# One pool of eight single PSUM banks in place of 3 + 4 + 1, with finer waits of the output projection

## The chip, the cores and the metric

The kernel runs on one core of a Trainium2 chip. The metric is the device time of one execution in microseconds (us). The core has a matrix engine (PE), a vector engine (DVE), a scalar engine (ACT), a further vector engine (POOL) and a queue for transfers (SP); they run side by side and wait for each other through semaphores. Matrix results land in PSUM, which this kernel uses as eight banks of 128 partitions x 512 float32; only after DVE or ACT has copied a bank out (evacuated it) can PE write it again.

## The reference, cut to what matters

Four layers on one sequence of 2048 rows of 576 columns: A, B, A, B, each added to its input after a normalization.

```python
def _A_ref(x, wqkv, wo):            # 32 heads of 18, window of 8 keys at distance 2
    ...
    logits = jnp.where(mask, jnp.einsum('bhsd,bhswd->bhsw', q, kg) * scale, -1e9)
    attn = _softmax(logits, axis=-1)
    o = jnp.einsum('bhsw,bhswd->bhsd', attn, vg)
    return o.transpose(0, 2, 1, 3).reshape(B, S, D) @ wo

def _B_ref(x, mem0, Wq, Wk, Wv, Wo, seg_len):   # 32 heads of 128, memory of 8 rows, segments of 32
    mem = mem0
    for s in range(n_seg):
        h = jnp.concatenate([mem, xs], axis=1)
        q, k, v = ...                            # three projections of h
        p = _softmax(jnp.where(mask, scores, -1e9), axis=-1)
        o = jnp.einsum('bhqk,bhke->bhqe', p, v)
        o = jnp.einsum('bhte,hed->btd', o, Wo)
        mem = o[:, :M, :].copy()                 # the next segment's memory
        outs.append(o[:, M:, :])

x = x + _A_ref(_layernorm(x), A_wqkv, A_wo)
x = x + _B_ref(_layernorm(x), B_mem0, B_Wq, B_Wk, B_Wv, B_Wo, B_seg_len)
x = x + _A_ref(_layernorm(x), A_wqkv, A_wo)
x = x + _B_ref(_layernorm(x), B_mem0, B_Wq, B_Wk, B_Wv, B_Wo, B_seg_len)
```

Layer B is a recurrence: the memory that a segment of 32 rows leaves is read by the next segment.

## The kernel before

All four layers run interleaved. Both B layers go on together as two "lanes": step t works on segment t of the first B layer and on segment t-6 of the second, so there are 64 + 6 = 70 steps (and one last projection). The A layers supply B with tiles of 64 rows, 32 tiles for each of two layers, 64 in all, so that two steps go by for two A tiles (one of each layer).

Every piece of work is recorded as an operation with an engine (or a choice of two: `AD_` is ACT or DVE), a cost, a priority and the buffers that it takes and frees. A planner (`_Plan.run`) then plays these through time with its own costs and writes the instructions out in the order that it finds; the numbers in `PR` are priorities. Each engine works through its written order strictly one instruction after the other.

A step of B (`b_step`) consists of:

- `qk`: eleven groups of up to three heads; a group fills one bank with queries and keys, and a copy by ACT or DVE takes it to SBUF (L731 and L733 on PE);
- `vpass`: values, two banks for each of three blocks (L776);
- `scores`: four of them (memory rows "m" and segment rows "x", each in two halves r = 0, 1), a softmax behind each (L809, L821; then L667 to L686 on DVE, ACT and POOL);
- `pv_m`, twice (r = 0, 1), and `pv_x`, once: probabilities times values (L845, L883). PE works in four groups of 32 rows of its array, and each group writes a bank of its own, so that four banks are taken at a time. The evacuations put the result into the SBUF tile `OT`, which has four parts c = 0 to 3 of eight heads each. `pv_x` of step t is used by the projection of step t+1;
- `oproj`: the output projection into one bank `psY`, as eight operations k = 0 to 7 of four heads each (L917); heads of operation k lie in part c = k mod 4, half r = k div 4, of `OT`;
- `mem_out`: three small copies on DVE from that bank into `hT`, the next step's input (L937 to L939). The first `qk` group of the next step waits for them. `x_out` adds the other rows to the residual (L959).

A tile of A (`a_tile`) has a normalization (L407), projections to q, k, v (L476), products on POOL, logits (L525), a softmax, and then `spread` (L550): 20 matmuls in four row groups copy the probabilities of 32 heads to the 18 rows of each head, into the tile `big`, which is then multiplied by v and summed on DVE and POOL, and projected (L582).

PSUM before is cut into three pools: `r` has three single banks, for everything but what follows; `o4` is one tile of four banks, for `pv_m`, `pv_x` and `spread`; `y` is one bank for `oproj`:

```python
self.pl.pool("r", [pp.tile([P, 512], F32, name=f"r{i}") for i in range(3)])
self.pl.pool("o4", [pp.tile([P, 4, 512], F32, name="o4")])
self.pl.pool("y", [pp.tile([P, 5, W80], F32, name="psY")])
```

So `pv_m`, `pv_x` and `spread` follow each other through one buffer: the next of them starts when all evacuations of the one before are done. `spread` takes it twice for a tile, with 16 and with 4 matmuls. Its evacuations copy one of five column blocks each, and read all four banks for it; those of `pv_x` copy one bank each; that of `pv_m` copies 64 columns of all four banks in one instruction.

The writing layer adds semaphore waits wherever two instructions of different engines touch the same tile; for a tile in PSUM it does so also where both only read it.

Of the kernel before, what the change touches and what calls it, by code (L numbers as in the profile page):

```python
# [16 lines left out]
P = 128  # L17
# [38 lines left out]
class _Plan:  # L56
# [36 lines left out]
    def run(self, log=None):  # L93
# [21 lines left out]
        while left:  # L115
            moved = True
            while moved:
                moved = False
                for e, heap in ready.items():
# [3 lines left out]
                    pick = None  # L123
                    while heap:
# [13 lines left out]
                        if all(len(self.pools[p]) >= k for p, k in need.items()):  # L138
                            pick = o
                            break  # L140
                        skipped.append(it)
# [63 lines left out]
class _K:  # L205
# [37 lines left out]
    def setup(self):  # L243
# [187 lines left out]
    def a_tile(self, layer, j, dep, due, span):  # L431
# [4 lines left out]
        def pr(f):  # L436
            return due - span * (1.0 - f)
# [108 lines left out]
        def spread(ps, c0, nb):  # L546
            for c in range(nb):
                for g in range(NQ):
                    q4 = slice(g * AH, (g + 1) * AH)
                    nc.tensor.matmul(ps.t[:, g, c * P:(c + 1) * P], lhsT=self.epadT[q4, c0 + c, :],  # L550
                                     rhs=e_.t[q4].rearrange("p w t -> p (w t)"), start=True, stop=True, skip_group_check=True)
        ps = pl.buf("o4")
        b = pl.op("PE", 0.35, lambda e, ps=ps: spread(ps, 0, 4), pr(Q[4]), [o], acq=[ps], uses=[e_], mode="R")
        evs = []
        for c in range(5):
            if c == 4:
                ps = pl.buf("o4")
                b = pl.op("PE", 0.1, lambda e, ps=ps: spread(ps, 4, 1), pr(Q[4] + 0.02), [b], acq=[ps], uses=[e_], mode="R")
            evs.append(pl.op(AD_, _evac(512),
                             lambda e, c=c, ps=ps: self.copy(e, big.t[:, c].rearrange("p w (g t) -> p g w t", g=NQ),  # L560
                                                             ps.t[:, :, c % 4 * P:(c % 4 + 1) * P].rearrange("p g (w t) -> p g w t", w=AW)),
                             pr(Q[4] + 0.01 * c), [b], uses=[ps, big]))
        mus = []
        for c0, nb in ((0, 2), (2, 2), (4, 1)):
            mus.append(pl.op("DVE", 0.15 + 0.3 * nb,
                             lambda e, c0=c0, nb=nb: self.tt(e, big.t[:, c0:c0 + nb], big.t[:, c0:c0 + nb], win(vT.t, c0, nb), ALU.mult),
                             pr(Q[5]), evs[c0:c0 + nb] + [got[2], got[2, "h"]], uses=[big, vT], lk=True))
# [268 lines left out]
    def pv_m(self, t, r, prio):  # L836
        nc, pl = self.nc, self.pl
        ps, (pt, dep), V = pl.buf("o4"), self.PT["m", r], self.vs(t)
# [253 lines left out]
```

## Time and profile before

| | |
|---|---|
| median of three runs | 2525.39 us (2518.47 to 2528.63) |
| profiled execution | 2515.65 us, its span 2513.9 us |
| granted clock of PE | 0.989 |
| busy: PE, DVE, ACT, POOL | 2178.0, 1449.9, 1173.8, 845.5 us |
| matmuls | 70664 |

The page shows for each engine its busy time; the time between is idle, and a further view gives, for each engine and line, what ended the idle time ("waited for"), with the total, the number of waits and the longest. "issue" there means that the engine waited for nothing that the profile shows. In the view of instructions in order of time, a row has its start and length in us, engine, line, operation, `written<-read` tiles, shape, a count, and in brackets the idle time before it with its releaser. The tile `o4` has the name `o` there, since numbers at the end of a name are left out; `r` stands for any of the three banks.

### The profile page before, as it was taken

The numbers are of one execution on the slowest core, as the hardware profiler recorded it, in microseconds if no ns is written. First come the engines' busy times: TensorE is split into PE (matmuls) and PEld (weight loads), VectorE is DVE, ScalarE is ACT, GpSimd is POOL, SyncE is SP. The second block draws the span as 40 slices with busy tenths as digits, with TensorE's granted clock in tenths as the row PEclk, the third lists the DMA queues.
The fourth block names the chain that finished last, engine by engine and source line by source line (L and its number), as shares of the span: only waits on it lengthen the run. The fifth ranks groups of instructions, "written<-read, shape, count | busy, mean of one in ns | idle before, by whom it ended". The sixth has DMA issues, their size and how long they took to land.

```text
span 2513.9 us, 153081 instructions
## 1 busy us (share of the span) xinstructions
PE 2178.0 (87%) x70664; PEld 1864.2 (74%) x70664; DVE 1449.9 (58%) x3510; ACT 1173.8 (47%) x2633; POOL 845.5 (34%) x1205
## 2 busy tenths in 40 slices
PE   0178889999999999999988999999999999999988
PEld 0167777778878777787877877788777887777776
DVE  1046656666566666666566666566566666665554
ACT  0034444455545554545544554445545455444443
POOL 4232442333333333233333333323333333332320
PEclk9999989999999999999999999999999999999999
DMA  7732333334344333333333433433343433322210
GB/s 249 206 118 85 114 99 99 98 106 121 110 117 117 108 103 114 103 109 103 113 114 113 121 103 96 116 100 106 105 119 108 122 112 107 99 81 64 64 50 10
DMA packets 231399, 270.11 MB, mean 107 GB/s; under 512 B 42340, under 2 KB 227236, under 8 KB 229220
## 3 DMA queue, kind: packets, MB, share of 16 engines
q1 hardware_dynamic: 227508, 241.44, 33.1%
q0 software_dynamic: 3248, 18.88, 2.2%
q8 instruction: 552, 9.04, 1.5%
q14 instruction: 91, 0.75, 0.1%
HBM read 244.10 MB, written 16.12 MB: 104 GB/s over the span
## 4 chain that ended last, share of the span: by engine, by line
PE 69%; DVE 12%; ACT 7%; issue 6%; SPq 3%; POOL 2%; DMA 1%; ACTq 0%; DVEq 0%; POOLq 0%
PE r L731 23%; PE psY L917 15%; PE r L776 8%; PE r L733 6%; PE r L476 6%; DVE big L235 3%; ACT big L233 3%; SPq L308 3%; PE o L883 3%; DVE r L668 2%; DVE nmx L667 2%; PE o L845 2%; PE r L582 2%; ACT OT L233 2%; ACT em L670 2%
## 5 line engine op out<-in xcount | busy, mean ns | idle before, releaser
L731 PE MATMUL r<-hT,wk 128*128 128x80 bf16 (+1 forms) x8960 | 678.2, 199 | 16.5 <-issue 16.4
L731 PE MATMUL r<-hT,wq 128*128 128x80 bf16 (+1 forms) x8960 | 678.6, 199 | 12.5 <-issue 8.2
L233 ACT ACTIVATE qk<-r 128x480 bf16<-128x480 f32 (+2 forms) x649 | 336.3, 519 | 319.5 <-PE r L733 305.9
L731 PEld LDWEIGHTS <-wq 128*128 128x128 bf16 x8960 | 453.7, 100 | 31.0 <-issue 24.3
L731 PEld LDWEIGHTS <-wk 128*128 128x128 bf16 x8960 | 456.1, 100 | 19.5 <-issue 19.5
L917 PE MATMUL psY<-OT,wo 128*128 128x80 bf16 (+3 forms) x11360 | 440.6, 199 | 30.1 <-ACT OT L233 13.3
L733 PE MATMUL r<-hT,wk_r 128*128 128x80 bf16 (+1 forms) x2240 | 446.1, 199 | 5.5 <-issue 5.5
L733 PE MATMUL r<-hT,wq_r 128*128 128x80 bf16 (+1 forms) x2240 | 446.0, 199 | 2.2 <-issue 2.2
L917 PEld LDWEIGHTS <-wo 128*128 128x128 bf16 x11360 | 414.0, 100 | 41.1 <-issue 40.1
L240 POOL TENSOR_TENSOR big<-qT,kT 128x1024 bf16<-128x1024 bf16 (+1 forms) x192 | 319.4, 1683 | 311.4 <-DVE oT L240 281.9
L776 PE MATMUL r<-wv,hT 128*32 128x512 bf16 x5408 | 355.9, 382 | 17.5 <-ACT em L670 12.0
L240 POOL TENSOR_TENSOR ex<-ex,sum 128x384 bf16<-128x384 bf16 x140 | 123.6, 883 | 609.1 <-DVE sum L678 312.6
L776 PEld LDWEIGHTS <-hT 128*32 128x32 bf16 x6760 | 172.7, 96 | 179.0 <-issue 40.5
L667 DVE TENSOR_REDUCE nmx<-r 128x4 f32<-128x320 f32 (+1 forms) x280 | 144.1, 515 | 200.2 <-PE r L821 188.9
L476 PE MATMUL r<-xn,ring 128*128 128x64 bf16 x4800 | 228.4, 195 | 22.0 <-issue 7.4
L233 ACT ACTIVATE OT<-o 128x256 bf16<-128x256 f32 (+1 forms) x276 | 133.1, 493 | 210.1 <-PE o L883 114.7
L733 PEld LDWEIGHTS <-wk_r 128*128 128x128 bf16 x2240 | 223.9, 100 | 5.3 <-issue 5.3
L733 PEld LDWEIGHTS <-wq_r 128*128 128x128 bf16 x2240 | 223.8, 100 | 3.9 <-issue 3.9
L476 PEld LDWEIGHTS <-ring 128*128 128x128 bf16 x4800 | 179.8, 99 | 55.9 <-issue 38.7
L233 ACT ACTIVATE V<-r 128x512 bf16<-128x512 f32 x306 | 179.7, 598 | 76.3 <-PE r L776 76.3
L240 POOL TENSOR_TENSOR big<-big 128x640 bf16<-128x640 bf16 (+1 forms) x39 | 62.9, 1613 | 334.7 <-DVE big L240 328.2
L235 DVE CAST big<-o 128x512 bf16<-128x512 f32 x131 | 90.5, 691 | 126.0 <-ACT big L233 64.9
(134 smaller groups left out, 3387.0 us busy)
## 6 DMA issues: line engine op xcount, KB each, us to landing
ring<-wA_blk SPq DMA_DIRECT2D x1280, 160.0 KB, 3.1
x1T<-x SPq DMA_DIRECT2D x32, 160.0 KB, 3.8
x<-x1T SPq DMA_DIRECT2D x32, 160.0 KB, 2.3
x3T<-x SPq DMA_DIRECT2D x32, 160.0 KB, 4.2
x<-x3T SPq DMA_DIRECT2D x32, 160.0 KB, 3.3
wo<-in_B_Wo_dram POOLq DMA_DIRECT2D x1, 4608.0 KB, 27.9
wq<-in_B_Wq_dram POOLq DMA_DIRECT2D x4, 1024.0 KB, 11.1
wk<-in_B_Wk_dram POOLq DMA_DIRECT2D x4, 1024.0 KB, 20.4
```

What stands on the lines that cost most here:

```text
L233: nc.scalar.activation(out=out, in_=in_, func=ACT.Copy, scale=1.0 if scale is None else scale)
L235: (nc.vector if e == "DVE" else nc.gpsimd).tensor_copy(out=out, in_=in_)
L240: (self.nc.vector if e == "DVE" else self.nc.gpsimd).tensor_tensor(out=out, in0=in0, in1=in1, op=op)
L308: nc.sync.dma_start(out=self.wA[i], in_=wn[:, :, col0:col0 + P])
L476: nc.tensor.matmul(ps.t[:, c * T:(c + 1) * T], lhsT=w.t[:, kc, :], rhs=xn.t[:, kc, :], start=(kc == 0), stop=(kc == 4))
L582: nc.tensor.matmul(ps.t[:, mb * T:(mb + 1) * T], lhsT=w.t[:, c, :], rhs=oT.t[:, c, :], start=(c == 0), stop=(c == 4))
L667: nc.vector.tensor_reduce(out=m, in_=v, axis=AX.X, op=ALU.max, negate=True)
L731: nc.tensor.matmul(pv[:, hh, wi, a:b], lhsT=wt[:, kc, h * P:(h + 1) * P], rhs=hT.t[:, kc, a:b], start=(kc == 0), stop=False)
L733: nc.tensor.matmul(pv[:, hh, wi, a:b], lhsT=wr[:, (h % 16) * P:(h % 16 + 1) * P], rhs=hT.t[:, 4 + h // 16, a:b], start=False, stop=True)
L776: nc.tensor.matmul(ps.t[c * 32:(c + 1) * 32, :], lhsT=l, rhs=w, start=(kc == 0), stop=(kc == 4))
L883: nc.tensor.matmul(o, lhsT=V[b].t[q4, r, i, :], rhs=p, start=(r == 0 and i == 0 and b == min(V)), stop=(r == 1 and i == 3 and b == 2), ski ...
L917: nc.tensor.matmul(psY.t[:, mb, c0:c1], lhsT=self.wo[:, w0:w0 + P], rhs=self.OT[:, h % 16 // 4 * 8 + h // 16 * 4 + h % 4, c0:c1], start=(h ...
```

## The change

The pools `o4` and `y` go; `r` has eight single banks, each a tile of its own. `pv_m`, `pv_x` and `spread` take any four of them, `oproj` any one.

`spread` runs as 8 and then 12 matmuls (2 and 3 of the five column blocks), each time into four banks. Each evacuation now copies one bank (256 or 384 columns, of a quarter of the times t) instead of one column block (512 columns out of four banks): four for each part, eight for a tile, where there were five.

`pv_m` is evacuated by four copies of 64 columns, one for each bank, instead of one of 256. An operation k of `oproj` waits for the `pv_x` copy of its own part c and the `pv_m` copy of its own part and half, instead of all of them. `pv_x` no longer waits for the evacuation of `pv_m` but for a marker behind `pv_m`'s first half.

The priorities `PR` have other values, so the order on all engines is another. The planner has a switch `HOLD`, which is off.

```diff
-        self.pl.pool("r", [pp.tile([P, 512], F32, name=f"r{i}") for i in range(3)])
-        self.pl.pool("o4", [pp.tile([P, 4, 512], F32, name="o4")])
-        self.pl.pool("y", [pp.tile([P, 5, W80], F32, name="psY")])
+        self.pl.pool("r", [pp.tile([P, 512], F32, name=f"r{i}") for i in range(8)])
...
-        ps = pl.buf("o4")
-        b = pl.op("PE", 0.35, lambda e, ps=ps: spread(ps, 0, 4), pr(Q[4]), [o], acq=[ps], uses=[e_], mode="R")
...
+        for n, (c0, nb) in enumerate(((0, 2), (2, 3))):
+            ps = [pl.buf("r") for _ in range(NQ)]
+            b = pl.op("PE", 0.09 * nb, lambda e, ps=ps, c0=c0, nb=nb: spread(ps, c0, nb), pr(Q[4] + 0.02 * n), [b], acq=ps,
+                      uses=[e_], mode="R")
+            evs[c0] = [pl.op(AD_, _evac(nb * P),
+                             lambda e, g=g, ps=ps, c0=c0, nb=nb: self.copy(
+                                 e, big.t[:, c0:c0 + nb, :, g * 16:(g + 1) * 16],
+                                 ps[g].t[:, 0:nb * P].rearrange("p (c w t) -> p c w t", c=nb, w=AW)),
+                             pr(Q[4] + 0.01 * n), [b], uses=[ps[g], big]) for g in range(NQ)]
...
+        for c in range(4):
+            s0 = 8 * c + 4 * r
+            self.om_ev.append(pl.op(AD_, _evac(64), lambda e, c=c, s0=s0: self.copy(
+                e, self.OT[:, s0:s0 + 4, MC:MC + 16], ps[c].t[:, 0:64].rearrange("p (i q) -> p i q", i=4)),
+                prio, [o, self.om_gate], uses=[ps[c], self.OTm]))
...
-        psY = self.psY = pl.buf("y")
+        psY = self.psY = pl.buf("r")
...
-            deps = [o] + (self.ox_ev if t > 0 else []) + ([self.om_ev[k // 4]] if m else [])
+            deps = [o] + ([self.ox_ev[k % 4]] if t > 0 else []) + ([self.om_ev[k]] if m else [])
...
-PR = dict(qk=0.116, qkd=0.051, v1=0.465, v0=0.812, m0=0.227, x0=0.46, m1=-0.024, x1=0.517, pm0=0.675, pm1=0.142,
+PR = dict(qk=0.102, qkd=0.032, v1=0.565, v0=1.428, m0=0.199, x0=0.438, m1=-0.279, x1=0.492, pm0=0.894, pm1=0.653,
...
+HOLD = False
```

The order on the engines, as it was written out, at three places. A row has its line (lines after the pools stand two to four higher in the changed kernel), the operation, `written<-read`, the size, and the semaphores that it waits for; numbers behind `r_` tell the banks apart.

On DVE, at the end of a step and the start of the next: `hT` are the copies of `mem_out`, then come the evacuations of `pv_x` into `OT`, those of `spread` into `big`, and the products. Before:

```order
L937 CAST hT_260<-psY 128x4x16 [waits PE_49]
L938 CAST hT_260<-psY 64x16
L939 CAST hT_260<-psY 64x16
L959 TENSOR_TENSOR x_305<-x_305,psY 128x5x32 [waits DMAHW7_49]
L959 TENSOR_TENSOR fin_333<-x_306,psY 128x5x32 [waits DMAHW7_49]
L235 CAST OT<-o_348 128x8x2x32 [waits Activation_49] x2
L235 CAST big_320<-o_348 128x4x8x16 [waits PE_49]
L235 CAST big_320<-o_348 128x4x8x16 [waits Activation_49]
L240 TENSOR_TENSOR big_320<-big_320,vT_315 128x1024 [waits DVE_49]
```

After, at the same place:

```order
L238 CAST big_320<-r_347 128x16x16 [waits PE_49]
L414 TENSOR_SCALAR st_310<-r_346 128x64 [waits PE_49,Activation_49]
L415 SCALAR_TENSOR_TENSOR st_310<-r_346,st_310 128x64 [waits DVE_49]
L416 SCALAR_TENSOR_TENSOR st_310<-r_346,st_310 128x64 [waits DVE_49]
L243 TENSOR_TENSOR big_320<-big_320,vT_315 128x1024 [waits Activation_49]
L238 CAST big_320<-r_349 128x24x16 [waits PE_49]
L238 CAST big_320<-r_347 128x24x16 [waits PE_49]
L941 CAST hT_260<-r_350 128x4x16 [waits PE_49]
L942 CAST hT_260<-r_350 64x16
L943 CAST hT_260<-r_350 64x16
L963 TENSOR_TENSOR x_305<-x_305,r_350 128x5x32 [waits DMAHW1_49]
L963 TENSOR_TENSOR fin_333<-x_306,r_350 128x5x32 [waits DMAHW7_49]
```

The evacuations of `spread`, and a product that waits for ACT's share of them, stand ahead of `mem_out` now; before, they stood behind it. The evacuations before wait for ACT, those after for PE alone.

On ACT, at `pv_m` in the middle of a step: `V` are evacuations of values. Before:

```order
L233 ACTIVATE V_272<-r_345 128x512 [waits PE_49]
L233 ACTIVATE big_320<-o_348 128x4x8x16 [waits DVE_49,PE_49,Pool_49]
L670 ACTIVATE em_265<-r_346 128x4x80 [waits DVE_49]
L233 ACTIVATE V_272<-r_345 128x512 [waits PE_49]
L233 ACTIVATE OT<-o_348 128x4x4x16 [waits PE_49]
L233 ACTIVATE qT_312<-r_346 128x320 [waits PE_49]
L670 ACTIVATE ex_269<-r_347 128x8x48 [waits DVE_49]
```

After:

```order
L236 ACTIVATE V_272<-r_348 128x512 [waits PE_49]
L236 ACTIVATE V_272<-r_346 128x512 [waits PE_49]
L236 ACTIVATE OT<-r_350 128x4x16 [waits PE_49]
L236 ACTIVATE OT<-r_352 128x4x16 [waits PE_49]
L236 ACTIVATE OT<-r_345 128x4x16 [waits PE_49]
L236 ACTIVATE OT<-r_351 128x4x16 [waits PE_49]
L236 ACTIVATE OT<-r_350 128x4x16 [waits PE_49]
L672 ACTIVATE ex_269<-r_347 128x8x48 [waits DVE_49]
```

Two evacuations of values now come together, straight ahead of the first small copies into `OT`, of which there are four for each `pv_m`.

More of the change, by code (lines that the diff above doesn't have):

```diff
@@ L123, in run @@
                     pick = None
+                    held = set()
                     while heap:
@@ L137, in run @@
                             break
-                        if all(len(self.pools[p]) >= k for p, k in need.items()):
+                        if all(len(self.pools[p]) >= k and p not in held for p, k in need.items()):
                             pick = o
                             break
+                        if HOLD:
+                            held.update(p for p, k in need.items() if k > 1 and len(self.pools[p]) < k)
                         skipped.append(it)
@@ L837, in pv_m @@
         nc, pl = self.nc, self.pl
-        ps, (pt, dep), V = pl.buf("o4"), self.PT["m", r], self.vs(t)
+        ps, (pt, dep), V = [pl.buf("r") for _ in range(4)], self.PT["m", r], self.vs(t)
         def mm(e):
@@ L934, in cp @@
         def cp(e):
-            y = psY.t
+            y = psY.t[:, 0:5 * W80].rearrange("p (c n) -> p c n", c=5)
             w = slice(MC + a, MC + b)
```

53 lines of the change are left out of this document (22 added, 31 removed).

## The prediction, on record before the changed kernel ran

> **What bounds the kernel now.** I read the page first, then what PE waited for, then the order of time at the places with the longest waits, and last the lengths by shape.
>
> From the page (the last line is a transfer queue: packets, MB, share of the transfer engines):
>
> ```profile
> span 2513.9 us, 153081 instructions
> PE 2178.0 (87%) x70664; PEld 1864.2 (74%) x70664; DVE 1449.9 (58%) x3510; ACT 1173.8 (47%) x2633; POOL 845.5 (34%) x1205
> ...
> PE 69%; DVE 12%; ACT 7%; issue 6%; SPq 3%; POOL 2%; DMA 1%; ACTq 0%; DVEq 0%; POOLq 0%
> ...
> q8 instruction: 552, 9.04, 1.5%
> ```
>
> PE is the bound: it is busy for 2178.0 of 2513.9 us and holds 69% of the chain that ended last. No other engine comes near, so a gain must come out of PE's 335.9 us of idle time. That is read from PE's waits (engine and line, what it waited for, total, number, longest):
>
> ```profile
> PE r L447 <- DMA x<-in_A_x_dram: 105.7, 2, 105.5
> PE o L550 <- DVE big L235: 31.5, 33, 2.0
> PE o L883 <- issue: 25.2, 23, 2.1
> PE r L731 <- issue: 24.5, 24, 2.6
> PE o L550 <- ACT big L233: 16.3, 28, 1.1
> PE psY L917 <- ACT OT L233: 13.3, 39, 1.1
> PE r L776 <- ACT em L670: 12.0, 38, 2.1
> PE psY L917 <- issue: 10.5, 18, 1.3
> ...
> PE r L733 <- issue: 7.7, 10, 1.5
> ...
> PE o L550 <- DVE OT L235: 7.3, 13, 0.6
> ```
>
> 105.7 us are the start, before the first rows of x are there; nothing of the change touches that. About 230 us are left. The three rows of L550 are `spread`, which waits for the four banks in which `pv_x` or its own first part still lies: 31.5 + 16.3 + 7.3 = 55.1 us in 74 waits. `vpass` waits 12.0 us in 38 waits for a bank that the exponential still reads, `oproj` 13.3 us in 39 waits for `OT`. These 80.4 us in 151 waits are what the change aims at. The four "issue" rows, 67.9 us, are no waits for a buffer.
>
> Why the four banks come free so late shows in the order of time, at the start of a step in the middle of the span. ACT, then DVE, then PE:
>
> ```profile
> 1376.57 0.60 ACT L233 ACTIVATE OT<-o 128x512 bf16<-128x512 f32 x1 [2.42 <-PE o L883]
> 1377.93 0.60 ACT L233 ACTIVATE OT<-o 128x512 bf16<-128x512 f32 x1 [0.76 <-DVE OT L235]
> ...
> 1380.48 0.60 ACT L233 ACTIVATE big<-o 128x512 bf16<-128x512 f32 x1 [0.78 <-DVE big L235]
> 1381.83 0.60 ACT L233 ACTIVATE big<-o 128x512 bf16<-128x512 f32 x1 [0.76 <-DVE big L235]
> ```
>
> ```profile
> 1377.20 0.69 DVE L235 CAST OT<-o 128x512 bf16<-128x512 f32 x1 [2.00 <-ACT OT L233]
> 1378.56 0.69 DVE L235 CAST OT<-o 128x512 bf16<-128x512 f32 x1 [0.66 <-ACT OT L233]
> 1379.75 0.69 DVE L235 CAST big<-o 128x512 bf16<-128x512 f32 x1 [0.51 <-PE o L550]
> 1381.11 0.69 DVE L235 CAST big<-o 128x512 bf16<-128x512 f32 x1 [0.66 <-ACT big L233]
> ```
>
> ```profile
> 1379.30 0.40 PE L550 MATMUL o<-e,epadT 32*128 32x128 bf16 x16 [0.58 <-DVE OT L235]
> ...
> 1380.51 0.39 PE L776 MATMUL r<-wv_r,hT 128*32 128x512 bf16 x4
> 1380.72 1.04 PE L776 MATMUL r<-wv,hT 128*32 128x512 bf16 x16
> 1381.59 0.39 PE L776 MATMUL r<-wv_r,hT 128*32 128x512 bf16 x4
> 1382.48 0.24 PE L550 MATMUL o<-e,epadT 32*128 32x128 bf16 x4 [0.50 <-ACT big L233]
> ```
>
> The reader is to see that ACT and DVE take turns: 1376.57, 1377.20, 1377.93, 1378.56, each copy begins when the other engine's ends. Four copies, two for each engine, take 1379.25 - 1376.57 = 2.68 us and not half of it, and the tile of four banks is held all that time. `spread` follows at 1379.30, its copies alternate again until 1382.43, and its second part follows at 1382.48. Over the span this turn-taking is seen in the waits of ACT and DVE:
>
> ```profile
> DVE OT L235 <- ACT OT L233: 84.0, 106, 2.7
> DVE big L235 <- ACT big L233: 64.9, 68, 3.3
> ACT big L233 <- DVE big L235: 63.3, 91, 1.0
> ACT OT L233 <- DVE OT L235: 50.3, 69, 1.7
> ```
>
> 262.5 us in all, in which two engines that do their lists in order hold back everything behind these copies.
>
> **The change part by part.** Lengths of the copies, by engine and shape:
>
> ```profile
> L233 ACT ACTIVATE V<-r 128x512 bf16<-128x512 f32 x306 | 179.7, 598 | 76.3 <-PE r L776 76.3
> L233 ACT ACTIVATE big<-o 128x512 bf16<-128x512 f32 x189 | 110.3, 599 | 89.2 <-DVE big L235 63.3 <-PE o L550 25.9
> L670 ACT ACTIVATE ex<-r 128x384 bf16<-128x384 f32 x140 | 68.6, 490 | 92.5 <-DVE r L668 87.3 <-PE r L476 0.9
> L233 ACT ACTIVATE OT<-o 128x256 bf16<-128x256 f32 x135 | 51.8, 384 | 74.9 <-PE o L845 44.5 <-PE o L883 25.1 <-DVE OT L235 4.7
> L233 ACT ACTIVATE ot<-r 64x64 bf16<-64x64 f32 x32 | 6.9, 217 | 14.7 <-PE r L627 14.7
> ```
>
> ```profile
> L235 DVE CAST qk<-r 128x480 bf16<-128x480 f32 x111 | 72.8, 656 | 56.1 <-PE r L733 55.1 <-PE r L821 1.0
> L240 DVE TENSOR_TENSOR big<-big,vT 128x1024 bf16<-128x1024 bf16 x128 | 88.0, 690 | 1.7
> L235 DVE CAST OT<-o 128x256 bf16<-128x256 f32 x53 | 22.1, 424 | 26.9 <-PE o L845 16.7 <-ACT OT L233 10.2
> ```
>
> (1) Banks one by one. A group of four no longer waits for one tile, and a copy no longer waits for the other engine's copy: in the new order the copies into `big` wait for PE alone, and many of those into `OT` too. Four copies of 256 columns, two on each engine, take some 2 x 0.42 = 0.85 us side by side, against 2.68 us in turns. With five more banks to choose from, `spread`, `vpass` and `oproj` lose the 80.4 us of idle time. The true loss is larger, since a row's length has PE's tail in it: a second `vpass` begins 0.21 us after the last row of the first (1380.51 to 1380.72), while `spread` begins 0.89 us after it (1381.59 to 1382.48), 0.68 us later than it could, of which 0.50 are shown idle. So 0.18 us come on top for each wait: 151 x 0.18 = 27 us. Together -107 us. The bounds are -107 and, if copies are still late when PE gets there, half of that.
>
> (2) More copies. `pv_m` comes twice in 70 steps, so 3 x 140 = 420 copies more, at about 0.22 us instead of a quarter of 0.384 each: 560 x 0.22 - 140 x 0.39 = 69 us of engine time. `spread` has 3 x 64 = 192 more: 256 at about 0.40 and 256 at about 0.52 (384 columns: 0.490 on ACT, between 0.424 and 0.656 on DVE), 236 us, against 110.3 us on ACT for 189 of the 320 copies and 131 on DVE, some 200 us together: +36. ACT and DVE are busy for 47% and 58% and lose 262.5 us of waits, which covers these 105 us. On the path I take 0. At best the first piece of `OT`, ready 0.384 - 0.217 = 0.17 us earlier, is what PE waits for, 70 times: -12 us. At worst, if a softmax on DVE sits in front of the small copies and the cover is gone, each `pv_m` is late by the three copies more, 0.65 us, in one of its two halves: 70 x 0.65 = +46 us. The first is nearer, since a piece of `oproj` needs one copy only.
>
> (3) New waits by the new order. Three show in it, one each in two steps, so some 32 to 35 times. `mem_out` on DVE has the product (0.690) and two copies of 384 columns (about 0.54 each) ahead of it, and the product waits for ACT's copies; PE has the rest of `oproj` and `pv_x` to do meanwhile. I put it 0.3 us late. The second part of `spread` follows the first after two `qk` groups, with DVE busy on a softmax: 0.3 us. `oproj` takes a bank that a `vpass` has just filled, whose copy on ACT is the second of two (2 x 0.598): 0.2 us. Sum 0.8 x 33 = 26 us. Bounds: 0, and the mean of the old waits for all three, (55.1/74 + 0.18) x 99 = 92 us.
>
> (4) The "issue" waits. They are where nothing else holds PE, 67.9 us in four rows, most at `pv_x` (23 waits of 1.1 us) and the `qk` behind it. 552 packets of 9.04 MB in all are 16 kB each, or, at 64 bytes for each of the 141328 matmuls and weight loads, 256 instructions; in 2400 us one comes every 4.35 us. `pv_x` is 96 very short matmuls with a weight load each, three quarters of such a block. My reading is that these waits are the arrival of PE's own instructions. If so, they don't go, and PE, spared other waits, catches up with the stream more often. I take a quarter more, +16 us; the bounds are 0 and a doubling, +68.
>
> [...]
>
> Sum: -107 + 26 + 16 = -65 us. On the profiled execution's own 2515.65 us this gives 2451; its median of three runs stands 9.7 us higher at 2525.39 and gives 2460. I say 2455. A difference of 0.5%, 13 us, is about what a measurement of this kernel can tell from no change.
>
> **The rivals.** *More than that.* The freed 262.5 us on ACT and DVE bring every other copy forward, the new waits of (3) don't come and neither does (4): -107, about 2410. For it speaks that banks of `qk` are reused after several groups now instead of two. Against it: a row of waits seldom goes without a successor.
>
> *The instruction stream takes it.* If (4) doubles, -107 + 26 + 68 = -13: 2505 to 2512. It decides when blocks come no faster than they are used now, one in 4.35 us. For it: the "issue" rows are the longest left. Against it: the waits of L550 lie beside `qk` and `vpass`, which use instructions slowly, so they don't hide much of the stream's.
>
> *Slower, by `mem_out`.* It closes the recurrence: if DVE comes to it late, the first `qk` of the next step starts late, and nothing else can be put there. With the product waiting for ACT's copies, and those for a normalization's work on ACT, it could be 2 to 3.5 us late in every second step. Above (107 - 16)/35 = 2.6 us it eats the gain; at 3.5 us it costs 122 - 91 = +31 us: about 2555. Against it: the copies wait for PE only and are short, and PE has twice 20 and once 40 matmuls of `oproj` between.
>
> *It doesn't do what it says*: the copies into one tile `big` or `OT` still alternate, since some rows keep a wait for the other engine. Then only `oproj` and `vpass` gain, 25 us less the small copies: about 2515. The order speaks against it for `big`.
>
> **How the numbers follow.** The forecast has 0.60, with its own range from 2425 to 2490 (the ends of (3) and (4) not both reached). More than that 0.17, the stream 0.08, slower by `mem_out` 0.10, not what it says 0.05. Faster by over 0.5% (below about 2513): 0.60 + 0.17 and half of the stream, 0.81. Within 0.5%: half of the stream and what it doesn't do, 0.09. Slower: 0.10. The range reaches from 2405 to 2512 and leaves out the slow rival and part of the last.
>
> **What would show it.** Of (1): the waits of `spread` (L551) gone from PE's list or under 20 us; ACT and DVE copying into `OT` and `big` at the same time, and the four rows of 262.5 us under 80. Of (2): ACT busy for some 60 us more, DVE for 40. Of (3): rows of PE waiting for DVE `hT` or ACT `V` under 30 us. Of (4): "issue" as the largest of PE's waits, 70 to 100 us in its main rows. The prediction is wrong if PE's idle time beside the start doesn't fall from 230 to some 160 us, or if it falls and PE's busy time rises instead.

## The result, and the profile after

The changed kernel takes 2418.0 us (median of four runs, 2416.32 to 2422.56), the kernel before 2526.89 in the same comparison: a ratio of 0.9578, with a 95% interval of 0.9553 to 0.9604. That is 109 us less; the forecast said some 65 to 70 less. The full range, 2405 to 2512, holds the result; the forecast's own, 2425 to 2490, does not. The profiled execution of the changed kernel took 2422.56 us, the longest of its four, so the two profiles differ by 93 us and not by 109.

From the page of the changed kernel, the lines that answer to those of before:

```profile
span 2420.9 us, 153998 instructions
PE 2160.7 (89%) x70664; PEld 1841.1 (76%) x70664; DVE 1453.2 (60%) x3697; ACT 1170.5 (48%) x3056; POOL 857.0 (35%) x1207
...
q8 instruction: 552, 9.04, 1.6%
...
PE 87%; issue 5%; SPq 3%; DMA 2%; POOL 1%; DVE 1%; ACT 0%; POOLq 0%; ACTq 0%; DVEq 0%
```

The last of these is the chain that ended last. DVE and ACT held 19% of it before and hold 1% now; PE went from 69% to 87%. PE's idle time fell from 335.9 to 260.2 us (-75.7), and its busy time by 17.3 us: together the 93.0 us of the span. What PE still waits for (same columns as before: total, number, longest):

```profile
PE r L448 <- DMA x<-in_A_x_dram: 105.2, 1, 105.2
PE r L733 <- issue: 30.5, 29, 2.4
PE r L921 <- issue: 20.5, 28, 2.3
PE r L887 <- issue: 18.8, 24, 1.8
PE r L847 <- issue: 13.9, 20, 1.5
PE r L477 <- DMA ring<-wA_blk: 11.7, 15, 3.9
...
PE r L921 <- ACT OT L236: 4.0, 10, 0.5
...
PE r L551 <- ACT big L236: 0.4, 1, 0.4
...
PE r L733 <- DVE hT L941: 0.3, 1, 0.3
```

The start is as long as it was. The waits of `spread` (L551) for a bank or its input, 55.1 us before, are 1.1 us in all; those of `vpass` for a bank of the exponential, 12.0 us, are gone; those of `oproj` for `OT` fell from 13.3 to 4.4. The largest part of what is left beside the start is "issue": 107 us over all its rows, 89 before.

ACT and DVE in order of time, at the evacuation of one `pv_x`:

```profile
1332.15 1.08 ACT L236 ACTIVATE OT<-r 128x512 bf16<-128x512 f32 x2 [2.04 <-PE r L887]
```

```profile
1332.18 1.29 DVE L238 CAST OT<-r 128x512 bf16<-128x512 f32 x2 [0.34 <-PE r L887]
```

Two copies on each engine, begun 0.03 us apart, and each waits for PE. The four are done at 1333.47, 1.32 us after the first began; before, the same four took 2.68 us in turns. Over the span this shows in what ACT waits for at these copies, and DVE (the longest row of each):

```profile
ACT OT L236 <- PE r L847: 97.8, 78, 3.9
```

```profile
DVE big L238 <- PE r L551: 70.8, 65, 3.1
```

Of the four rows in which these copies waited for the other engine, 262.5 us, none is left. A copy that waits for PE costs nothing here: it is early, and PE is the engine that bounds the kernel.

### The profile page after: what moved, and what is told of

The parts are those of the page before. It is cut to its first block, busy times and chain, and to the rows that moved or that the text cites. A ratio compares the mean times of both kernels' runs of the same rounds, so it can differ in the third digit from the quotient of the medians.

```text
span 2420.9 us, 153998 instructions
## 1 busy us (share of the span) xinstructions
PE 2160.7 (89%) x70664; PEld 1841.1 (76%) x70664; DVE 1453.2 (60%) x3697; ACT 1170.5 (48%) x3056; POOL 857.0 (35%) x1207
## 4 chain that ended last, share of the span: by engine, by line
PE 87%; issue 5%; SPq 3%; DMA 2%; POOL 1%; DVE 1%; ACT 0%; POOLq 0%; ACTq 0%; DVEq 0%
PE r L733 26%; PE r L921 16%; PE r L778 15%; PE r L477 6%; PE r L735 6%; SPq L311 3%; PE r L887 3%; PE r L847 2%; PE r L823 2%; PE r L584 2%; PE r L811 2%; DMA ring<-wA_blk 2%; PE r L408 2%; PE r L551 1%; PE r L526 1%
## 5 line engine op out<-in xcount | busy, mean ns | idle before, releaser
L733 PE MATMUL r<-hT,wq 128*128 128x80 bf16 (+1 forms) x8960 | 677.3, 199 | 16.5 <-issue 13.7
L733 PE MATMUL r<-hT,wk 128*128 128x80 bf16 (+1 forms) x8960 | 676.4, 199 | 16.8 <-issue 16.8
L733 PEld LDWEIGHTS <-wq 128*128 128x128 bf16 x8960 | 451.1, 100 | 55.8 <-issue 50.0
L733 PEld LDWEIGHTS <-wk 128*128 128x128 bf16 x8960 | 454.2, 100 | 17.3 <-issue 17.3
L921 PE MATMUL r<-OT,wo 128*128 128x80 bf16 (+3 forms) x11360 | 436.6, 199 | 25.4 <-issue 20.5
L921 PEld LDWEIGHTS <-wo 128*128 128x128 bf16 x11360 | 406.7, 99 | 38.4 <-issue 29.8
L243 POOL TENSOR_TENSOR ex<-ex,sum 128x384 bf16<-128x384 bf16 x140 | 118.5, 847 | 507.7 <-DVE sum L680 436.9
L236 ACT ACTIVATE V<-r 128x512 bf16<-128x512 f32 x331 | 197.4, 596 | 201.7 <-PE r L778 199.4
L778 PEld LDWEIGHTS <-hT 128*32 128x32 bf16 x6760 | 163.2, 96 | 141.9 <-issue 7.3
L477 PE MATMUL r<-xn,ring 128*128 128x64 bf16 x4800 | 224.4, 196 | 22.9 <-DMA ring<-wA_blk 11.7
L236 ACT ACTIVATE OT<-r 128x64 bf16<-128x64 f32 (+2 forms) x586 | 144.1, 312 | 174.0 <-PE r L847 97.8
L477 PEld LDWEIGHTS <-ring 128*128 128x128 bf16 x4800 | 176.0, 99 | 59.8 <-issue 36.8
L670 DVE TENSOR_TENSOR r<-r,nmx 128x320 f32<-128x320 f32 (+1 forms) x280 | 149.1, 533 | 9.6
```

Of the source, the lines that this page charges most:

```text
L236: nc.scalar.activation(out=out, in_=in_, func=ACT.Copy, scale=1.0 if scale is None else scale)
L243: (self.nc.vector if e == "DVE" else self.nc.gpsimd).tensor_tensor(out=out, in0=in0, in1=in1, op=op)
L477: nc.tensor.matmul(ps.t[:, c * T:(c + 1) * T], lhsT=w.t[:, kc, :], rhs=xn.t[:, kc, :], start=(kc == 0), stop=(kc == 4))
L670: nc.vector.tensor_tensor(out=v, in0=v, in1=m.unsqueeze(len(shp) - 1).to_broadcast(shp), op=ALU.add)
L733: nc.tensor.matmul(pv[:, hh, wi, a:b], lhsT=wt[:, kc, h * P:(h + 1) * P], rhs=hT.t[:, kc, a:b], start=(kc == 0), stop=False)
L778: nc.tensor.matmul(ps.t[c * 32:(c + 1) * 32, :], lhsT=l, rhs=w, start=(kc == 0), stop=(kc == 4))
```

## The experiments

Two readings of the gain are weighed in the texts on record. Theory A: it comes from banks that are evacuated and freed one by one, so that ACT and DVE no longer take turns. Theory B: it comes from the pool, eight banks that anything may take. Beside them stand the finer waits, the new priorities, and the question what "issue" is. Ratios are to the kernel before on the same chip (its medians there: 2513.87, 2518.95 and 2523.44 us), and differences in us are worked out from the ratios with these medians.

**The banks alone.** The pools stay three, four and one; only the four banks become tiles of their own, with what hangs on it: `spread` as 8 and 12 matmuls, four small copies for each `pv_m`, and `pv_x` behind the marker. Old priorities, and each operation of `oproj` waits for all copies of `pv_x` and of its half of `pv_m`.

```diff
-        self.pl.pool("o4", [pp.tile([P, 4, 512], F32, name="o4")])
+        self.pl.pool("o4", [pp.tile([P, 512], F32, name=f"o{i}") for i in range(4)])
...
-            deps = [o] + (self.ox_ev if t > 0 else []) + ([self.om_ev[k // 4]] if m else [])
+            deps = [o] + (self.ox_ev if t > 0 else []) + (self.om_ev[4 * (k // 4):4 * (k // 4) + 4] if m else [])
```

> The kernel before with one part of the change: the four banks of pv_m, pv_x and spread are four tiles, evacuated and freed one by one (spread as 8 + 12 matmuls, pv_m by four small copies), in a pool of their own; r keeps its three banks, y its one, the priorities and the projection's coarse waits are those of before. Theory A (the end of the turn-taking between ACT and DVE on one tile is what counts): the waits of spread fall from 55 us to under 20, the four rows of ACT and DVE waiting for each other from 262 to under 100, and 50 to 75 us are gained, 2450 to 2475; vpass and the projection keep their waits of 12 and 13 us. Theory B (the number of banks to choose from counts, and with it the longer time until a bank is used again): under 25 us, 2500 or more. Theory C (the new priorities count): no gain, 2515 to 2535.

Measured: 2465.97 us, ratio 0.9805 (0.9785 to 0.9825), 49 us less than before and a bit under half of the gain. No row is left in which ACT and DVE wait for each other's copies into `OT` and `big`: the 262.5 us of turns are gone with the banks alone. What PE waits for:

```profile
PE r L780 <- ACT em L674: 29.2, 37, 2.4
...
PE psY L923 <- ACT OT L236: 4.3, 11, 0.6
```

`spread` waits no more here either, and `oproj` little. But `vpass` (L780 in this kernel), still with three banks to choose from, waits 29.2 us for the bank that the exponential reads, 12.0 before: part of what the banks gave came back there. In the kernels with one pool, also with the old priorities, that row is gone; this is what B adds.

**The pool with one bank less.** The changed kernel with seven banks.

```diff
-        self.pl.pool("r", [pp.tile([P, 512], F32, name=f"r{i}") for i in range(8)])
+        self.pl.pool("r", [pp.tile([P, 512], F32, name=f"r{i}") for i in range(7)])
```

> The changed kernel with seven banks in the pool instead of eight. Theory A (the end of the turn-taking is what counts): within 10 us of the changed kernel. Theory B (banks to choose from): each bank counts, 15 to 40 us are lost, with waits of PE for ACT and DVE copies back in its list.

Measured: 2451.48 us, ratio 0.973 (0.9701 to 0.9759). The eighth bank is worth 1.5%, some 38 us. PE waits again for evacuations, at places where it did not:

```profile
PE r L477 <- ACT big L236: 9.8, 26, 0.7
PE r L921 <- ACT OT L236: 8.1, 21, 0.7
...
PE r L477 <- ACT ex L672: 7.5, 19, 0.7
PE r L408 <- ACT V L236: 6.7, 26, 0.3
```

These are short waits, 92 of 0.35 us in the mean, 32.1 us in all. But they don't make PE's idle time longer: "issue" fell from 107.0 to 67.0 us, and all idle time from 260.2 to 249.5. What shows in the profile is PE's busy time, 2191.2 us, 30.5 more. The order is another too with seven banks: in the trace PE changes the shape of its tiles 1352 times, 1163 times with eight, and each change costs about 0.10 us (below, at the masks). So the 38 us are the price of the bank and of its order together, and not a sum of waits for banks.

**The old priorities.** All of the change but the table `PR`.

```diff
-PR = dict(qk=0.102, qkd=0.032, v1=0.565, v0=1.428, m0=0.199, x0=0.438, m1=-0.279, x1=0.492, pm0=0.894, pm1=0.653,
+PR = dict(qk=0.116, qkd=0.051, v1=0.465, v0=0.812, m0=0.227, x0=0.46, m1=-0.024, x1=0.517, pm0=0.675, pm1=0.142,
...
```

> The changed kernel with the priorities of the kernel before. Theory A or B: nearly all of the 109 us stay, 2415 to 2440. Theory C: more than half is lost, over 2475.

Measured: 2428.55 us, ratio 0.9649 (0.9629 to 0.9669), 88 us less than before. The new priorities bring the last 0.7%, some 18 us, so most of the gain does not hang on them. In its waits one row stands out that the changed kernel has at 4.0 us:

```profile
PE r L921 <- ACT OT L236: 26.2, 64, 0.8
...
PE r L847 <- DVE ptm L688: 7.9, 8, 1.7
```

The new priorities put other work of PE between `pv_m` and the piece of `oproj` (L921) that needs it, as in this place of the changed kernel:

```profile
1320.42 0.51 PE L847 MATMUL r<-ptm,V 32*128 32x16 bf16 x48
...
1321.26 0.46 PE L526 MATMUL r<-big,epad 128*32 128x128 bf16 x20
...
1321.81 1.60 PE L921 MATMUL r<-OT,wo 128*128 128x80 bf16 x40
```

But PE's idle time as a whole is 250.5 us with the old priorities and 260.2 with the new, since "issue" is 65.1 us against 107.0; its busy time is 16.4 us longer. So the wait for `OT` is not the 18 us; what they are is open.

**The finer waits, on the kernel before.** Only those of `pv_x`, since `pv_m` has one copy there.

```diff
-            deps = [o] + (self.ox_ev if t > 0 else []) + ([self.om_ev[k // 4]] if m else [])
+            deps = [o] + ([self.ox_ev[k % 4]] if t > 0 else []) + ([self.om_ev[k // 4]] if m else [])
```

> The kernel before with the finer waits of the projection on the pv_x copies alone (operation k waits for the copy of its own part). By the waits before (13.3 us of the projection for OT, 39 times) at most 13 + 39 x 0.18 = 20 us; theory A says that the copies of pv_x alternate on a tile and are long done by then, so that 0 to 8 us are gained: 2515 to 2525. A gain of over 15 us would say that the finer waits are a main part of the change.

Measured: 2518.59 us, ratio 1.0004 (0.9987 to 1.0022): nothing. The wait it might have shortened stands as it was:

```profile
PE psY L917 <- ACT OT L233: 13.0, 39, 0.7
```

**The finer waits, on the changed kernel.** First the waits of `pv_x` made coarse again, with the new priorities:

```diff
-            deps = [o] + ([self.ox_ev[k % 4]] if t > 0 else []) + ([self.om_ev[k]] if m else [])
+            deps = [o] + (self.ox_ev if t > 0 else []) + ([self.om_ev[k]] if m else [])
```

> The changed kernel, in which each operation of the projection waits for all four pv_x copies instead of its own part's; the pv_m waits stay fine. pv_x is done some twenty us before the projection, so that its copies are long over: no change, 0.956 to 0.962, if the wait itself is what counts. If the planner's order depends on it: anything else, and then the order on PE differs.

Measured: 2415.35 us, ratio 0.9569 (0.9538 to 0.96), as the changed kernel. `pv_x` belongs to the step before and is long evacuated (in the changed kernel, with both lanes on, its last copy into `OT` ends 16 to 25 us before the next `oproj` begins); the planner writes PE's instructions in the same order. Next, with the old priorities, both kinds coarse:

```diff
-            deps = [o] + ([self.ox_ev[k % 4]] if t > 0 else []) + ([self.om_ev[k]] if m else [])
+            deps = [o] + (self.ox_ev if t > 0 else []) + (self.om_ev[4 * (k // 4):4 * (k // 4) + 4] if m else [])
```

> The changed kernel with the priorities of before and with the projection's coarse waits (each operation waits for all pv_x copies and for the four pv_m copies of its half). With those priorities and the finer waits the ratio was 0.965, and PE waited 26 us for OT in 64 waits. If the finer waits matter once the other waits are gone: 15 to 40 us more, 0.971 to 0.981, which is where the four single banks alone came out (0.9805). If they don't: 0.962 to 0.968, and what is between the two came from the pool of eight.

Measured: 2534.17 us, ratio 1.0067 (1.0042 to 1.0091). The whole gain is gone, which is outside of both outcomes that were expected, though `spread` hardly waits. Then only those of `pv_m` coarse, old priorities:

```diff
-            deps = [o] + ([self.ox_ev[k % 4]] if t > 0 else []) + ([self.om_ev[k]] if m else [])
+            deps = [o] + ([self.ox_ev[k % 4]] if t > 0 else []) + (self.om_ev[4 * (k // 4):4 * (k // 4) + 4] if m else [])
```

> The changed kernel with the priorities of before, and the projection waiting for all four pv_m copies of its half; the pv_x waits stay fine. With all waits coarse the ratio was 1.007, with all fine 0.965. If the pv_m waits are what counts (they lie right ahead of the projection): about 1.00, with a granted clock of 0.97 again. If the pv_x waits do: about 0.965.

Measured: 2544.68 us, ratio 1.0082 (1.0056 to 1.0108). So under the old priorities it is the waits of `pv_m` that count, 4% of the time. What PE waits for with both kinds coarse:

```profile
PE r L847 <- DVE ptm L688: 34.1, 32, 2.2
PE r L408 <- ACT xs L402: 32.6, 30, 1.4
...
PE r L921 <- ACT OT L236: 2.2, 5, 0.8
```

The kernel with the old priorities and fine waits has 7.9 and 6.6 us in the first two rows, and 26.2 in the last: PE waits less for `OT` with coarse waits than with fine ones, so the waits of `oproj` for its copies are not what costs. The order differs. PE at `pv_m` in the kernel with coarse waits:

```profile
1261.48 0.38 PE L408 MATMUL r<-xs,ones 128*128 128x128 bf16 x4 [1.06 <-ACT xs L402]
...
1261.85 0.57 PE L847 MATMUL r<-ptm,V 32*128 32x16 bf16 x48
1263.49 0.51 PE L847 MATMUL r<-ptm,V 32*128 32x16 bf16 x48 [1.06 <-DVE ptm L688]
1263.93 4.26 PE L921 MATMUL r<-OT,wo 128*128 128x80 bf16 x70
```

And in the one with fine waits:

```profile
1282.14 0.88 PE L921 MATMUL r<-OT,wo 128*128 128x80 bf16 x20
...
1283.42 2.31 PE L921 MATMUL r<-OT,wo 128*128 128x80 bf16 x60
1285.67 0.51 PE L847 MATMUL r<-ptm,V 32*128 32x16 bf16 x48
1286.53 3.03 PE L921 MATMUL r<-OT,wo 128*128 128x80 bf16 x80 [0.35 <-ACT OT L236]
```

With fine waits, 80 matmuls of `oproj` (20 and 60) stand ahead of this half of `pv_m`, behind the other half. With coarse ones nothing stands between the two halves, and only the sums of a normalization (L408) right ahead of them, and PE waits twice for 1.06 us within 4 us. The second loss is in the last row of the first of the two fences: 70 matmuls in 4.26 us, 61 ns each, against 80 in 3.03, 38 ns each. The trace has 40 falls of PE's granted clock, all to 0.50, and all begin on one grid of 3.41 us. Two stretches of that grid at the two waits, then two at the place where the same pair stands again (1334.62 and 1336.62), with length and PE's busy time at the front and the granted clock in the column before the last two:

```profile
1260.56:1263.97 3.41, 1.43 (x103) 1.22 (x102) 3.20 (x10) 2.80 (x11) 1.07 (x2) 1.00 0.02 5
1263.97:1267.38 3.41, 3.41 (x56) 3.41 (x54) 2.81 (x10) 0.83 (x3) 2.01 (x2) 0.50 0.00 0
...
1332.23:1335.64 3.41, 2.27 (x84) 1.38 (x74) 3.24 (x9) 2.40 (x7) 0.00 (x0) 1.00 0.02 5
1335.64:1339.06 3.42, 2.44 (x104) 2.42 (x105) 3.17 (x9) 1.80 (x9) 1.77 (x2) 1.00 0.00 0
```

At the first place both waits lie, but for 0.14 us, in one stretch of the grid: PE is busy for 1.43 of 3.41 us, and for the next 3.41 us its clock is granted at 0.50. At the second the border of the grid, 1335.64, lies between the waits, PE is busy for 2.27 and 2.44 us, and the clock stays. Between 400 and 2500 us of this trace, each of the 18 stretches of the grid at full clock in which PE is busy for less than half is followed by such a fall; from half to three quarters it goes either way. In the changed kernel, whose falls lie on such a grid too, a stretch from 1160.63 us, with PE busy for 1.61 of 3.41 us, is followed by none. So the same pair of waits cost clock at the one place, and not at the other, where the border of the grid fell between them.

The mean clock of this kernel is 0.967 and that of the other with coarse `pv_m` waits 0.956, against 0.992 with fine waits. The books close: its span is 104.9 us longer than with fine waits and old priorities, PE's busy time 53.7 us of it (2230.8 against 2177.1) and the idle time 51.2. The clock stands at 0.50 for 168.0 us here and for 42.8 there; 125 us more at half the pace (in the changed kernel a matmul of 128x80 begins 36 ns behind one of its own shape at full clock, and 67 ns at 0.50) are up to 63 us of busy time, an estimate that covers the 53.7. Two waits of 1.06 us were enough for a fall where they lay, but for 0.14 us, in one stretch of the grid; behind the first 130 us PE's longest wait in this trace is 2.6 us.

Why the planner leaves that place empty with coarse waits isn't settled, and the two kernels that would part wait and order (coarse waits of `pv_m` with the new priorities, and the new priorities on the old pools) have no run.

**What "issue" is.** 5120 very short matmuls behind the end of the changed kernel, in two bursts of 2560, the second beside 48 loads of A's weights:

```diff
...
+        burst()
+        for w in ring[0:2]:
+            nc.scalar.activation(out=w[:, 0, 0:32], in_=ps[3][:, 480:512], func=ACT.Copy, scale=1.0)
+        burst()
+        for n in range(48):
+            nc.sync.dma_start(out=ring[n % 2][:], in_=self.wA[n % WOB])
```

> The changed kernel with work added at its end that no output uses: 2560 short matmuls of 32 rows x 32 columns, four row groups in four banks as in pv_x (5120 instructions with the weight loads, 20 blocks of 256), then copies by ACT, and the same 2560 again while SP loads 48 blocks of A's weights, some 0.5 in a us. If the issue waits are PE's instructions arriving, the first burst takes about 20 x 3.5 = 70 us instead of the 23 us that the spacing of 8 to 9 ns in pv_x gives, with waits named issue at every 128th matmul, and the second is longer by 5 to 30 us, since the transfers share the engines that bring the instructions. If they are something else (PE's own pace, a semaphore), both bursts take 23 to 30 us.

Measured: 2551.06 us in one run. PE in order of time, the first burst above, the second below:

```profile
2408.62 1.23 PE L1004 MATMUL r<-ident 32*128 32x32 bf16 x128 [2.25 <-issue]
2412.09 1.22 PE L1004 MATMUL r<-ident 32*128 32x32 bf16 x128 [2.25 <-issue]
...
2493.01 1.22 PE L1004 MATMUL r<-ident 32*128 32x32 bf16 x128 [3.34 <-issue]
2497.57 1.22 PE L1004 MATMUL r<-ident 32*128 32x32 bf16 x128 [3.34 <-issue]
```

Nothing here waits for a buffer, and PE stops after every 128 matmuls: with their weight loads 256 instructions, one block of 16 kB. The queue of instructions has 592 packets of 9.70 MB in this kernel, 40 packets and 0.66 MB more than in the changed one, for the 10240 instructions of the bursts. PE does a block in 1.22 us and waits 2.25 for the next: a block every 3.47 us at best, without loads up to 4.03 and 3.68 in the mean (2401.40 to 2460.26, 16 blocks), with the loads beside it 3.75 to 4.57, from 2468.04 to 2543.98 18 blocks or 4.22 us each. The page shows a granted clock of 0.5 from 2422 us to the end, which holds most of both bursts; the waits are no work of PE. The reading of "issue" as the arrival of PE's own instructions is shown for a stream as dense as this. It also says where the changed kernel stands: its 552 blocks in the 2316 us behind the start are one every 4.19 us.

**The loads taken away.** The changed kernel with only the first six of the 1280 loads of A's weights; all later tiles of A are computed with what those left. PE's instructions and their order are the same.

```diff
+        def ld(e):
+            self.loads = getattr(self, "loads", 0) + 1
+            if self.loads <= 6:
+                self.nc.sync.dma_start(out=w.t[:], in_=self.wA[i])
...
```

> The changed kernel without the repeated loads of A's weight blocks (only the first six of 1280 are made, and the result is that of stale weights): same instructions on PE, but some 205 MB less of transfers. If the instructions' arrival holds PE and shares the transfer engines (3.5 us a block with them quiet, about 4.1 with loads beside it), PE's issue rows fall from 107 us to under 60 and 40 to 90 us are gained. If it doesn't, only PE's waits for the loads go, 12 us and their tails: 10 to 18 us.

Measured: 2326.99 us, ratio 0.9236 (0.9209 to 0.9262), 3.4% or 86 us less than the changed kernel. PE's waits for these loads, 11.7 us at L477 and 0.8 at L584, explain a small part. The rest is in

```profile
PE r L737 <- issue: 19.4, 32, 1.4
PE r L891 <- issue: 7.7, 14, 1.0
```

All "issue" rows together are 44.6 us here and 107.0 with the loads. The spans differ by 97.5 us: 62.4 of "issue", 12.5 of waits for the loads, and 22.6 of PE's busy time, for which no run here gives a cause. So transfers for which PE waits only 12.5 us slow the arrival of its instructions here, by 62.4 us of "issue".

**Fewer instructions.** The mask is added to the scores by one matmul of 128 columns instead of four of 32; 840 matmuls fewer.

```diff
-            for c in range(4):
-                msk = self.mask_m[:].unsqueeze(1).to_broadcast([P, 4, W80]) if m else \
-                    self.mask_x[:].unsqueeze(2).to_broadcast([P, 2, 4, 48])
-                nc.tensor.matmul(v[c * 32:(c + 1) * 32], lhsT=self.ident[:, 0:32], rhs=msk, start=True, stop=False,
...
+            nc.tensor.matmul(v, lhsT=self.ident[:, :], rhs=msk, start=True, stop=False, skip_group_check=True)
```

> The changed kernel; the mask of a score is added by one matmul over all 128 columns of PE's array instead of four that run side by side on 32 columns each. 840 matmuls and as many weight loads fall away, 1680 instructions or 6.6 blocks of 256, while PE's work lasts as long as before. If PE is held by the arrival of its instructions (2312 us for 552 blocks, 4.19 us each), 12 to 27 us are gained over the changed kernel: ratio to the kernel before 0.947 to 0.953 instead of 0.958. If PE is held by its matmuls' own time, nothing outside 5 us.

Measured: 2428.78 us, ratio 0.9635 (0.9607 to 0.9664): no gain. "Issue" did fall, to 76.9 us, but PE's busy time rose by 40.3 to 2201.0. PE at the scores in the changed kernel, then in this one:

```profile
1408.77 0.31 PE L811 MATMUL r<-mask_m,ident 128*32 128x320 bf16 x4
1408.91 0.32 PE L823 MATMUL r<-qk 128*32 128x80 bf16 x16
```

```profile
1416.68 0.31 PE L812 MATMUL r<-mask_m,ident 128*128 128x320 bf16 x1
1416.92 0.33 PE L823 MATMUL r<-qk 128*32 128x80 bf16 x16
1417.18 0.34 PE L812 MATMUL r<-mask_x,ident 128*128 128x384 bf16 x1
```

The same shape of tile all along: the next group begins 0.14 us later. Alternating between 128*128 and 128*32, it is 0.24 and 0.26, about 0.11 us more for each change. The rest of the trace agrees: in the changed kernel, behind a matmul of 128*128 with 80 columns the next begins 36 ns later when its shape is the same and 132 to 134 ns later when it is another. PE changes shape 1163 times there and 1613 times here; 450 more at 0.10 us are 45 us, near the 40.3 measured. Another kernel sets both masks together, to save half of these changes; its diff beside the one above, with the old priorities:

```diff
...
+            if m:
+                nc.tensor.matmul(v, lhsT=self.ident[:, :], rhs=self.mask_m[:].unsqueeze(1).to_broadcast([P, 4, W80]),
+                                 start=True, stop=False, skip_group_check=True)
+                nc.tensor.matmul(psx.t[:, 0:384].rearrange("p (l i k) -> p l i k", l=2, i=4), lhsT=self.ident[:, :],
...
```

> The changed kernel with the priorities of before (ratio 0.965), with each mask added by one matmul of 128 columns, and the masks of the two scores of a half issued together ahead of both, so that PE's array changes its shape once for them instead of at each: 1680 instructions fewer as before, without most of the 40 us that the single change of the masks added to PE's busy time. If instructions are what holds PE: 10 to 25 us less than with the masks in four, 0.955 to 0.961. If changes of shape eat it again: 0.963 to 0.972.

Measured: 2435.89 us, ratio 0.9664 (0.9637 to 0.9691), against 0.9649 with the same priorities and the masks as they were: no gain either.

**The switch on.** With it, a bank is kept back for a group that wants four.

```diff
-HOLD = False
+HOLD = True
```

> The changed kernel with the planner's switch HOLD on: an operation that needs four banks keeps later ones off the pool until it has them. Priorities were set with the switch off. Theory B (banks to choose from): groups of four start earlier, others later; within 1% of the changed kernel, 0.950 to 0.968, with PE's issue rows still the largest.

Measured: 2453.23 us, ratio 0.972 (0.9693 to 0.9746), outside of what was expected, and 1.4% slower than without. PE waits again for banks at the operations that take four, `spread` and `pv_x`:

```profile
PE r L551 <- ACT big L236: 9.1, 22, 0.4
...
PE r L887 <- ACT big L236: 7.4, 25, 0.6
```

16.5 us in these two rows; but PE's idle time as a whole is only 3.7 us longer, and its busy time 26.3 us; the cause of that is open. Of the versions that do all the work none was clearly better than the changed kernel.

## Why the prediction was right, and where a term was off

(1) *Banks one by one, -107.* The mechanism was as told: the turns ended, and the three kinds of waits fell from 80.4 to 5.5 us, -74.9. PE's busy time fell by 17.3 us, where 27 were put for the tails that a row's length holds: -92 in place of -107. The four rows of turns were to be under 80 us and are gone. The 17.3 are no measure of the tails alone, though. PE changes the shape of its tiles 1031 times before and 1163 times after, which at 0.10 us each costs some 13 us that no term had, so the tails gave some 30 (an estimate). That this is near 27 is partly luck: at the place that the 0.18 us were read from, 0.10 of them is the change of shape between `vpass` and `spread`, which stays (in the kernel before, at the 33 places where work on tiles of 32*128, as `spread` is, follows `vpass` without a wait, it begins 0.31 us behind, not 0.21). And the banks as such give 49 us; the rest hangs on the pool, the finer waits and the order.

(2) *More copies, 0 on the path.* Right on the path. The engine time, 105 us, was too high by more than half: copies into `OT` and `big` are busy for 418.7 us before (217.9 and 200.8 on both engines) and 456.7 after, +38. The step took the mean length of a copy times the number. Copies that follow each other on one engine overlap: the 441 small ones on ACT have a mean of 233 ns and fill 70.6 us, not 103. As a whole ACT is busy 3.3 us less and DVE 3.3 more, not 60 and 40 more, since their other work takes about as much less.

(3) *New waits, +26.* They did not come. The row of `qk` waiting for `hT` has 0.3 us, no row of waiting for `V` is left, and the second part of `spread` has its share of 1.1 us. The step that failed read an order in which DVE comes to `mem_out` behind a product as a wait. DVE at that place, after:

```profile
1328.54 1.12 DVE L243 TENSOR_TENSOR big<-big,vT 128x1024 bf16<-128x1024 bf16 x1
1329.59 1.01 DVE L238 CAST big<-r 128x384 bf16<-128x384 f32 x2
1330.76 0.22 DVE L941 CAST hT<-r 128x64 bf16<-128x64 f32 x1 [0.16 <-PE r L921]
```

The product and both evacuations are done when PE ends `oproj`, and it is DVE that waits. Zero was the lower bound of the step, and the condition of "more than that".

(4) *"Issue", +16.* Right: 89 to 107 us, +18, with 100.3 in its six main rows; the reading behind it is shown by the two kernels above. In the burst PE waits 2.25 us per block at best, with no load beside it; in the changed kernel itself the waits are 107 us over 552 blocks, 0.19 us each.

The sum of these is -92 + 18 = -74; waits of other kinds and the gaps below what the list shows fell by another 18.2 us (60.7 to 42.5), which no term had, and the start by 0.5: the 93 us of the profiles. The medians differ by 16 us more, since the one profile lies 11 us below its median and the other 4.6 above. PE's idle time beside the start went from 230 to 155 us, 160 forecast. So the path was right and the sum too small: (1) came out 15 us short and (3) was 26 us of waits that did not come, two errors that partly cancel, which is luck; the 18 us of other waits were missing. The measured 2418 lies below the forecast's own range, in what was left to the rival "more than that" (about 2410). That rival was nearer, for the reason it gave in (3), but not in (4).

The rival in which the instruction stream takes the gain did not come true, since its condition did not hold: blocks come every 3.47 us at best and every 4.22 beside loads, faster than the 4.35 at which they were used. At 4.19 us a block in the changed kernel no margin is left by that figure. (By its own sum the rival's lower end is 2503 us, not 2505.) The rival of the late `mem_out` would have shown at L733, and doesn't.

What the prediction didn't see at all: how much hangs on the order. One pool with coarse waits and the old priorities is slower than before by 0.7%, while single banks in the old pools, with the same waits, are faster by 2%. The parts don't add. The banks' 49 us are shown by themselves; how the other half of the gain divides between the pool, the finer waits and the order is not.

## What to carry to other kernels

When two engines evacuate one tile of several PSUM banks, look for rows in which each waits for the other's copy; a tile for each bank removed 262.5 us of such waits here and by itself made the kernel 49 us shorter. Where a planner sets the order, measure each part of a change also in the full change, since a dependency for which PE waits 2 us in all can move work and cost 4%. When waits for nothing remain on PE, count its instructions in blocks of 256 and divide the time: this kernel stands at 4.19 us a block, the burst beside loads at 4.22, and of its 107 us of "issue" 62.4 went with loads for which PE waits only 12.5 us.

## What the hardware did that was not expected

- In a burst of very short matmuls a block of 256 instructions of PE arrives every 3.47 us at best, every 3.68 in the mean and every 4.22 beside loads; taking away 1274 loads made 70664 unchanged matmuls 86 us faster.
- Changing between tiles of 128*128 and 128*32 cost PE about 0.10 us each time (36 ns to the next matmul of the same shape, 132 to 134 to one of another); in the kernel with 450 more changes PE was busy for 40 us longer.
- PE's granted clock fell to 0.50 for 3.41 us behind two waits of 1.06 us, where both lay in one stretch of a grid of 3.41 us; over a kernel with 40 falls PE was busy for 53.7 us longer than over one with 10.
